# Column strips, split segments and a relaid order in a recurrent-memory attention block with a feed-forward layer

## The chip, the cores and the metric

The kernel runs on one core of a Trainium2 chip. The metric is the device time of one execution in microseconds (us). TensorE (PE; its weight loads are listed as PEld) does the matmuls, VectorE is DVE, ScalarE is ACT, GpSimd is POOL, SyncE (SP) issues transfers. The arrays are in bfloat16, sums in PSUM in float32.

## The reference

`x` has 2048 rows of D = 640. `_A_ref` walks 64 segments of 32 rows. Eight memory rows are put ahead of each segment, attention with 32 heads of 128 runs over these 40 rows, and the first eight rows of its output are the memory of the next segment. So the segments follow one another. `_B_ref` is a feed-forward layer with a squared relu.

```python
for s in range(n_seg):
    h = jnp.concatenate([mem, xs], axis=1)              # 8 + 32 rows
    q, k, v = h Wq, h Wk, h Wv                          # 32 heads of 128
    scores = jnp.einsum('bhqe,bhke->bhqk', q, k) * scale
    scores = jnp.where(mask[None, None], scores, -1000000000.0)
    p = _softmax(scores, axis=-1)
    o = jnp.einsum('bhte,hed->btd', p v, Wo)
    mem = o[:, :M, :].copy()
    outs.append(o[:, M:, :])
...
h = x + _A_ref(_layernorm(x), ...)
h2 = h + _B_ref(_layernorm(h), ...)                     # F = 1728
```

The mask lets the memory rows see all 40 rows, and a segment's row the memory and the rows up to itself.

## The kernel before, in words

There are three phases.

1. Layernorm of all of `x` (L97 to L111): 16 blocks of 128 rows are normalized, transposed on TensorE and written to DRAM as `xnT_dram`. Then the four weight matrices are loaded (L119 to L122), 5 MB each.
2. The recurrence (L140 to L246), a loop over pairs of segments, written as `step`. `hT` holds the transposed rows of a segment, 32 from `xnT_dram` and 8 of memory. For q and k (L154), a block of the weights is the stationary operand (128 x 128) and the 40 columns of `hT` stream through it: 320 weight loads and 320 matmuls of 40 columns. For v (L191), `hT` is stationary (40 columns of the array used) and the weights stream in pieces of 512. Scores are made head by head (L178), scaled and masked on DVE (L180); softmax (L194 to L200) takes the maximum, subtracts, exponentiates on ACT, sums, and multiplies by the reciprocal. The probabilities are transposed (L212), multiplied with v (L220), and Wo is applied with the 40 columns of `oT` stationary (L233). Eight of the result's rows go through `memsb` (L236) and a transpose (L133, L135) into the next segment's `hT`; the others are added to `x` (L240) and written to DRAM as `h1_dram`.
3. The feed-forward layer (L265 to L297): for each block of 128 rows, layernorm, transpose, first product (L281), relu on ACT (L284), square on DVE (L285), second product (L291), bias (L293) and residual (L296).

[...] The framework places the instructions on each engine's queue and adds the semaphores.

Of the kernel before, what the change touches and what calls it, by code (L numbers as in the profile page):

```python
# [16 lines left out]
def kernel(  # L17
# [16 lines left out]
    nc = tc.nc  # L34
# [4 lines left out]
    L = SEG + M  # L39
    NSEG = S // SEG  # L40
    DC = D // 128
    F = B_w1.shape[1]
# [6 lines left out]
    GRP = [(0, 12), (12, 12), (24, 8)]  # L49
    HALF = D // 2  # L50
# [9 lines left out]
    h1_dram = dram.tile([S, D], BF16)  # L60
    xnT_dram = dram.tile([128, DC, S + SEG], BF16)
# [4 lines left out]
    mask = const.tile([L, L], F32)  # L66
    nc.gpsimd.memset(mask[:], 0.0)
    nc.gpsimd.affine_select(out=mask[:, 0:SEG], in_=mask[:, 0:SEG], compare_op=ALU.is_ge, fill=-1e9,
                            base=0, pattern=[[-1, SEG]], channel_multiplier=1)
    mask32 = const.tile([L, H, L], F32)  # L70
    for h in range(H):
        nc.gpsimd.tensor_copy(out=mask32[:, h, :], in_=mask[:])

# [3 lines left out]
    def layernorm(pool, src, n, dst, tagp):  # L77
        xf = pool.tile([128, D], F32, tag=tagp + "xf")
        nc.vector.tensor_copy(out=xf[:n], in_=src)  # L79
        FMAX = nc.vector.BN_STATS_FMAX  # L80
        nsub = 1
        while D // nsub > FMAX or D % nsub:
            nsub += 1
        st = pool.tile([128, nsub, nc.vector.BN_STATS_DIM], F32, tag=tagp + "st")
        xr = xf[:n].rearrange("p (s f) -> p s f", s=nsub)
        for s_ in range(nsub):
            nc.vector.bn_stats(out=st[:n, s_, :], in_=xr[:, s_, :])  # L87
        mv = pool.tile([128, nc.vector.BN_AGGR_DIM], F32, tag=tagp + "mv")
        nc.vector.bn_aggr(out=mv[:n], in_=st[:n])
        rstd = pool.tile([128, 1], F32, tag=tagp + "rs")  # L90
        nc.scalar.activation(out=rstd[:n], in_=mv[:n, 1:2], func=ACT.Sqrt, bias=eps_t[:n], scale=1.0)
        nc.vector.reciprocal(out=rstd[:n], in_=rstd[:n])
        nc.vector.tensor_scalar(out=dst, in0=xf[:n], scalar1=mv[:n, 0:1], scalar2=rstd[:n, 0:1],
                                op0=ALU.subtract, op1=ALU.mult)

    with tc.tile_pool(name="p0", bufs=2) as p0:
        zt = p0.tile([128, DC, SEG], BF16, tag="zt")  # L97
        nc.vector.memset(zt[:], 0.0)
        nc.gpsimd.dma_start(out=xnT_dram[:, :, S:S + SEG], in_=zt[:])
        for g in range(S // 128):  # L100
            xt = p0.tile([128, D], BF16, tag="xt")
            (nc.sync if g % 2 == 0 else nc.scalar).dma_start(out=xt[:], in_=x2d[g * 128:(g + 1) * 128, :])
            xn0 = p0.tile([128, D], BF16, tag="xn0")
            layernorm(p0, xt[:], 128, xn0[:], "ln0")
            pt0 = psum_t.tile([128, 1024], BF16, tag="pt")
            ptv0 = pt0[:, 0:DC * 128].rearrange("p (c m) -> p c m", m=128)
            for c in range(DC):
                nc.tensor.transpose(out=ptv0[:, c, :], in_=xn0[:, c * 128:(c + 1) * 128], identity=ident[:])
            xT0 = p0.tile([128, DC, 128], BF16, tag="xT0")
            nc.vector.tensor_copy(out=xT0[:], in_=ptv0)  # L110
            nc.gpsimd.dma_start(out=xnT_dram[:, :, g * 128:(g + 1) * 128], in_=xT0[:])  # L111

    with tc.tile_pool(name="wts", bufs=1) as wts, tc.tile_pool(name="sb", bufs=1) as sb, \
            tc.tile_pool(name="sm", bufs=2) as sm:
# [4 lines left out]
        nc.sync.dma_start(out=wq[:], in_=A_Wq.rearrange("(c p) h e -> p c (h e)", p=128))  # L119
        nc.scalar.dma_start(out=wk[:], in_=A_Wk.rearrange("(c p) h e -> p c (h e)", p=128))  # L120
        nc.gpsimd.dma_start(out=wv[:], in_=A_Wv.rearrange("(c p) h e -> p c (h e)", p=128))
        nc.sync.dma_start(out=wo[:], in_=A_Wo.rearrange("h e d -> e h d"))  # L122

        hT_a = wts.tile([128, DC, L], BF16)
        hT_b = wts.tile([128, DC, L], BF16)
        memsb = wts.tile([L, D], BF16)
        nc.scalar.dma_start(out=memsb[SEG:L, :], in_=A_mem0[0])

        def mem_to_hT(hT):
            pt = psum_t.tile([128, 1024], BF16, tag="pt")  # L130
            ptv = pt[:, 0:DC * M].rearrange("p (c m) -> p c m", m=M)
            for c in range(DC):
                nc.tensor.transpose(out=ptv[:, c, :], in_=memsb[SEG:L, c * 128:(c + 1) * 128],  # L133
                                    identity=ident[SEG:L, SEG:L])
            nc.vector.tensor_copy(out=hT[:, :, SEG:L], in_=ptv)  # L135

        mem_to_hT(hT_a)
        nc.sync.dma_start(out=hT_a[:, :, 0:SEG], in_=xnT_dram[:, :, 0:SEG])

        def step(t0, off, hT, hT_next):  # L140
            nc.gpsimd.dma_start(out=hT_next[:, :, 0:SEG], in_=xnT_dram[:, :, ds(t0 + (off + SEG), SEG)])
            xs = sm.tile([SEG, D], BF16, tag="xs")
            nc.sync.dma_start(out=xs[:], in_=x2d[ds(t0 + off, SEG), :])

            qT = sb.tile([128, H, L], BF16, tag="qT")
            kT = sb.tile([128, H, L], BF16, tag="kT")
            ei = 0
            for (w_sb, dstT) in ((wq, qT), (wk, kT)):
                for (h0, nh) in GRP:
                    ps = psum.tile([128, 512], F32, tag="mm")  # L150
                    for hl in range(nh):
                        h = h0 + hl
                        for c in range(DC):
                            nc.tensor.matmul(ps[:, hl * L:(hl + 1) * L], lhsT=w_sb[:, c, h * E:(h + 1) * E],  # L154
                                             rhs=hT[:, c, :], start=(c == 0), stop=(c == DC - 1))
                    src = ps[:, 0:nh * L].rearrange("p (h l) -> p h l", l=L)
                    if ei % 2 == 0:
                        nc.vector.tensor_copy(out=dstT[:, h0:h0 + nh, :], in_=src)  # L158
                    else:
                        nc.scalar.copy(out=dstT[:, h0:h0 + nh, :], in_=src)  # L160
                    ei += 1
            v_sb = sb.tile([L, HE], BF16, tag="v")

            HC = 16
            HB = 8
            oT = sb.tile([128, H, L], BF16, tag="oT")
            s = sb.tile([L, H, L], F32, tag="s")
            p = sb.tile([L, H, L], BF16, tag="p")
            pT = sb.tile([L, H, L], BF16, tag="pT")
            mx = sm.tile([L, H], F32, tag="mx")  # L170
            sume = sm.tile([L, H], F32, tag="sume")
            rs = sm.tile([L, H], F32, tag="rsum")
            for b in range(H // HB):
                h0 = b * HB
                ps = psum.tile([128, 512], F32, tag="mm")
                for hl in range(HB):
                    h = h0 + hl
                    nc.tensor.matmul(ps[0:L, hl * L:(hl + 1) * L], lhsT=qT[:, h, :], rhs=kT[:, h, :],  # L178
                                     start=True, stop=True)
                nc.vector.scalar_tensor_tensor(out=s[:, h0:h0 + HB, :],  # L180
                                               in0=ps[0:L, 0:HB * L].rearrange("p (h l) -> p h l", l=L),
                                               scalar=scale, in1=mask32[:, h0:h0 + HB, :],
                                               op0=ALU.mult, op1=ALU.add)
            NVG = HE // 512 // (H // HC)
            for ch in range(H // HC):
                hs = slice(ch * HC, (ch + 1) * HC)
                vps = []
                for n in range(ch * NVG, (ch + 1) * NVG):
                    psv = psum.tile([128, 512], F32, tag="mm", name="vps%d" % n)
                    for c in range(DC):  # L190
                        nc.tensor.matmul(psv[0:L, :], lhsT=hT[:, c, :], rhs=wv[:, c, n * 512:(n + 1) * 512],  # L191
                                         start=(c == 0), stop=(c == DC - 1))
                    vps.append((n, psv))
# [8 lines left out]
                for (n, psv) in vps:  # L202
                    if n % 2 == 0:
                        nc.vector.tensor_copy(out=v_sb[:, n * 512:(n + 1) * 512], in_=psv[0:L, :])  # L204
                    else:
                        nc.scalar.copy(out=v_sb[:, n * 512:(n + 1) * 512], in_=psv[0:L, :])  # L206
# [125 lines left out]
```

## Time and profile before

| | before |
|---|---|
| time, median of 4 | 2596.22 us (2595.84 to 2596.57) |
| profiled span | 2594.5 us |
| TensorE busy | 2155.7 us, 83% |
| DVE busy | 1098.5 us, 42% |
| ACT busy | 607.4 us, 23% |
| mean granted TensorE clock | 0.911 of full speed |

A share of busy time is a mean over phases with different limits. In the rows of groups, `x4096` is the count, then come the total busy time in us, the mean of one in ns, and the idle time of the engine just before. A matmul's listed time runs from its start to its result, so neighbours overlap; what one costs in a row of many is the distance between two starts.

### The profile page before, as it was taken

The numbers are of one execution on the slowest core, as the hardware profiler recorded it, in microseconds if no ns is written. First come the engines' busy times: TensorE is split into PE (matmuls) and PEld (weight loads), VectorE is DVE, ScalarE is ACT, GpSimd is POOL, SyncE is SP. The second block draws the span as 40 slices with busy tenths as digits, with TensorE's granted clock in tenths as the row PEclk, the third lists the DMA queues.
The fourth block names the chain that finished last, engine by engine and source line by source line (L and its number), as shares of the span: only waits on it lengthen the run. The fifth ranks groups of instructions, "written<-read, shape, count | busy, mean of one in ns | idle before, by whom it ended". The sixth has DMA issues, their size and how long they took to land. (4 is left out here: it accounts for less than half of the span.)

```text
span 2594.5 us, 77532 instructions
## 1 busy us (share of the span) xinstructions
PE 2155.7 (83%) x35333; PEld 1568.4 (60%) x35333; DVE 1098.5 (42%) x2262; ACT 607.4 (23%) x1138; POOL 102.5 (4%) x141
## 2 busy tenths in 40 slices
PE   1388889888888888988888888889888888888688
PEld 1266666666566665666666666666666566665465
DVE  6243344433444334444344443344433444334465
ACT  1121222212222122222122221222212222122354
POOL 3000000000000000000000000000000000000011
PEclk9998899888898989989888998899988889989899
DMA  5600000000000000000000000000000000000210
GB/s 178 231 5 6 6 4 5 6 6 6 5 6 6 5 6 6 3 6 6 6 6 5 6 5 6 6 4 5 6 6 6 6 5 6 5 6 13 83 35 29
DMA packets 25770, 49.07 MB, mean 19 GB/s; under 512 B 4984, under 2 KB 21056, under 8 KB 23536
## 3 DMA queue, kind: packets, MB, share of 16 engines
q1 hardware_dynamic: 17984, 24.55, 3.1%
q0 software_dynamic: 3888, 10.70, 1.6%
q10 hardware_dynamic: 3584, 8.78, 0.9%
q8 instruction: 302, 4.95, 0.8%
q14 instruction: 12, 0.10, 0.0%
HBM read 36.10 MB, written 7.91 MB: 17 GB/s over the span
## 5 line engine op out<-in xcount | busy, mean ns | idle before, releaser
L233 PE MATMUL pso<-wo,oT 128*40 128x320 bf16 x4096 | 648.9, 326 | 0.0
L233 PEld LDWEIGHTS <-oT 128*40 128x40 bf16 x4096 | 439.7, 109 | 190.6
L154 PEld LDWEIGHTS <-wq 128*128 128x128 bf16 x10240 | 300.4, 102 | 178.8 <-issue 178.1
L236 DVE CAST memsb<-pso 8x320 bf16<-8x320 f32 x128 | 56.6, 478 | 604.2 <-PE pso L233 604.2
L154 PE MATMUL ps<-hT_a,wq 128*128 128x40 bf16 x5120 | 166.0, 196 | 165.0 <-PEq L244 149.4
L191 PE MATMUL vps<-wv,hT_a 128*40 128x512 bf16 x1280 | 281.4, 379 | 0.0
L191 PE MATMUL vps<-wv,hT_b 128*40 128x512 bf16 x1280 | 281.4, 379 | 0.0
L154 PEld LDWEIGHTS <-wk 128*128 128x128 bf16 x10240 | 264.6, 96 | 0.1
L158 DVE CAST qT<-ps 128x480 bf16<-128x480 f32 (+1 forms) x128 | 73.5, 575 | 395.5 <-PE ps L154 395.5
L206 ACT CAST v_sb<-vps 40x512 bf16<-40x512 f32 x256 | 147.0, 574 | 289.3 <-PE vps L191 289.3
L191 PEld LDWEIGHTS <-hT_b 128*40 128x40 bf16 x1280 | 125.4, 100 | 141.0
L191 PEld LDWEIGHTS <-hT_a 128*40 128x40 bf16 x1280 | 125.4, 100 | 141.0
L160 ACT CAST qT<-ps 128x480 bf16<-128x480 f32 x64 | 35.7, 558 | 656.6 <-PE ps L154 656.6
L204 DVE CAST v_sb<-vps 40x512 bf16<-40x512 f32 x256 | 168.9, 660 | 0.0
L160 ACT ACT_TABLE_LOAD x32 | 41.1, 1283 | 454.1 <-PEq L244 446.8
L154 PE MATMUL ps<-hT_b,wq 128*128 128x40 bf16 x5120 | 137.4, 181 | 11.7 <-DVE hT_b L135 11.7
L154 PE MATMUL ps<-hT_b,wk 128*128 128x40 bf16 x5120 | 135.4, 180 | 0.0
L154 PE MATMUL ps<-hT_a,wk 128*128 128x40 bf16 x5120 | 134.6, 180 | 0.0
L180 DVE SCALAR_TENSOR_TENSOR s<-ps,mask 40x320 f32<-40x320 f32 x256 | 107.3, 475 | 44.7 <-PE ps L178 44.7
L160 ACT CAST kT<-ps 128x480 bf16<-128x480 f32 (+1 forms) x128 | 62.9, 492 | 254.0 <-PE ps L154 254.0
L226 DVE CAST oT<-ps 128x320 bf16<-128x320 f32 x128 | 63.0, 492 | 138.1 <-PE ps L220 138.1
L212 PE MATMUL pt<-ident,p 40*40 40x40 bf16 x2048 | 83.5, 178 | 43.0 <-DVE p L200 43.0
(64 smaller groups left out, 1804.4 us busy)
## 6 DMA issues: line engine op xcount, KB each, us to landing
wq<-in_A_Wq_dram SPq DMA_DIRECT2D x1, 5120.0 KB, 37.6
wk<-in_A_Wk_dram ACTq DMA_DIRECT2D x1, 5120.0 KB, 38.9
wo<-in_A_Wo_dram SPq DMA_DIRECT2D x1, 5120.0 KB, 55.7
wv<-in_A_Wv_dram POOLq DMA_DIRECT2D x1, 5120.0 KB, 40.5
xnT_dram<-xT POOLq DMA_DIRECT2D x16, 160.0 KB, 2.7
xs<-in_A_x_dram SPq DMA_DIRECT2D x64, 40.0 KB, 1.7
h_dram<-h SPq DMA_DIRECT2D x64, 40.0 KB, 1.9
ht<-h_dram SPq DMA_DIRECT2D x16, 160.0 KB, 2.4
```

The lines of the kernel that those rows point to most:

```text
L154: nc.tensor.matmul(ps[:, hl * L:(hl + 1) * L], lhsT=w_sb[:, c, h * E:(h + 1) * E], rhs=hT[:, c, :], start=(c == 0), stop=(c == DC - 1))
L158: nc.vector.tensor_copy(out=dstT[:, h0:h0 + nh, :], in_=src)
L160: nc.scalar.copy(out=dstT[:, h0:h0 + nh, :], in_=src)
L180: nc.vector.scalar_tensor_tensor(out=s[:, h0:h0 + HB, :], in0=ps[0:L, 0:HB * L].rearrange("p (h l) -> p h l", l=L), scalar=scale, in1=mask ...
L191: nc.tensor.matmul(psv[0:L, :], lhsT=hT[:, c, :], rhs=wv[:, c, n * 512:(n + 1) * 512], start=(c == 0), stop=(c == DC - 1))
L204: nc.vector.tensor_copy(out=v_sb[:, n * 512:(n + 1) * 512], in_=psv[0:L, :])
L206: nc.scalar.copy(out=v_sb[:, n * 512:(n + 1) * 512], in_=psv[0:L, :])
L212: nc.tensor.transpose(out=pt2[0:L, hl * L:(hl + 1) * L], in_=p[:, h, :], identity=ident[0:L, 0:L])
L226: nc.vector.tensor_copy(out=oT[:, h0:h0 + HB, :], in_=src)
L233: nc.tensor.matmul(pso[hf][0:L, 0:HALF], lhsT=oT[:, h, :], rhs=wo[:, h, hf * HALF:(hf + 1) * HALF], start=(h == 0), stop=(h == H - 1))
L236: nc.vector.tensor_copy(out=memsb[SEG:L, hf * HALF:(hf + 1) * HALF], in_=pso[hf][SEG:L, 0:HALF])
```

## The change

The change rewrites the recurrence around a narrower stationary operand. It is meant to put four 32-row products into the array side by side and to fill the waits of the recurrence with work that doesn't depend on the memory.

- *Strips.* Heads fall into four groups of eight (G = 4, EG = 1024 columns). The 32 stationary columns of a segment's rows are loaded into four column strips of the array; strip g streams the weights of its own head group and writes PSUM partitions 32g to 32g+31. This holds for q, k and v alike (L185).
- *Split segments.* The 32 stationary rows are the 8 memory rows and the first 24 of a segment (HD = 24). The last eight rows (TL = 8) never feed a later segment's memory other than as keys and values, and their q, k and v don't depend on the memory. The last eight rows of four segments make one 32-row tail pass per block of 128 rows, done one block ahead.
- *Transposes.* q and k are transposed by `turn` (L198), four 128-column transposes at a time.
- *Scores* (L288 to L298): the masks are brought into PSUM by products with the identity, then 64 products of 40 and of 16 columns add the scores. Exp has no subtraction of the maximum. The sums over keys come from a product with a block matrix of ones (L304, L305); the reciprocal is Exp of minus Ln, on ACT.
- *p times v* (L322, L326): 64 products with 32 rows each, in four row groups and four PSUM banks.
- *Wo* for memory and first rows (L338): 16 sets of four strips with 320 columns. This product goes over the even heads alone, and strip g streams the 320 columns of its pair g//2, of which the first 160 are copied out; the odd heads' share of the sum is not formed. As many columns are streamed as 32 heads of 160 would need. Tail rows have all heads (L205).
- *Order.* TensorE's order is as written in the source; `run_fill` takes pieces of the list `fill` (tail passes, their transposes, the tail's Wo, the next block's layernorm transposes) at four places of a step. All 64 steps are written out, without a loop. Layernorm of a block comes just ahead of its use, and its root is Exp of -0.5 times Ln, so that one function table serves all.
- *DRAM.* Attention outputs go to `o_main` and `o_tail`; the feed-forward phase reads them back with `x`, in tiles of 512 rows, w1 stationary and 512 columns streaming.

```diff
-            for (w_sb, dstT) in ((wq, qT), (wk, kT)):
-                for (h0, nh) in GRP:
-                    for hl in range(nh):
-                        for c in range(DC):
-                            nc.tensor.matmul(ps[:, hl * L:(hl + 1) * L], lhsT=w_sb[:, c, h * E:(h + 1) * E],
-                                             rhs=hT[:, c, :], start=(c == 0), stop=(c == DC - 1))
+        def pass_units(w, lhs, n, ps, c0=0, c1=DC):
+            for c in range(c0, c1):
+                for g in range(G):
+                    nc.tensor.matmul(ps[32 * g:32 * g + 32, :], lhsT=lhs(c),
+                                     rhs=w[:, c, g * EG + n * 512:g * EG + (n + 1) * 512],
+                                     start=(c == 0), stop=(c == DC - 1))
...
+        def main_step(b, sp):
+            nc.gpsimd.tensor_copy(out=qT[:, :, :, 0:TL], in_=tl["q"][:, :, :, sp * TL:(sp + 1) * TL])
+            half(wq, lhs, 0, qr, "act")
+            half(wq, lhs, 1, qr, "dve")
+            half(wk, lhs, 0, kr, "act")
+            turn(qr, 0, qT[:, 0:4, :, TL:NQ], "dve")
+            half(wk, lhs, 1, kr, "dve")
+            turn(qr, 1, qT[:, 4:8, :, TL:NQ], "act")
+            half(wv, lhs, 0, vr, "act")
+            turn(kr, 0, kT[:, 0:4], "dve")
+            turn(kr, 1, kT[:, 4:8], "act")
+            half(wv, lhs, 1, vr, "dve")
...
+            p = s1.tile([128, PM + PT], BF16, tag="p")
+            nc.scalar.activation(out=p[:], in_=ps[:, 0:PM + PT], func=ACT.Exp, scale=scale)
+            run_fill(3)
...
+            nc.scalar.activation(out=lz[:], in_=pz[:, 0:PM], func=ACT.Ln)
+            nc.scalar.activation(out=rz[:], in_=lz[:], func=ACT.Exp, scale=-1.0)
+            nc.vector.tensor_tensor(out=pn[:, 0:PM], in0=p[:, 0:PM], in1=rz[:], op=ALU.mult)
...
+            run_fill(5)
...
+            run_fill(3)
+            pw = psum.tile([128, 512], F32, tag="mm", name="pw")
+            for h in range(0, H, 2):
+                for g in range(G):
+                    nc.tensor.matmul(pw[32 * g:32 * g + 32, 0:2 * DG], lhsT=oT[:, h, TL:NQ],
+                                     rhs=wo[:, h, (g // 2) * 2 * DG:(g // 2 + 1) * 2 * DG],
+                                     start=(h == 0), stop=(h == H - 2))
+            o = s3.tile([128, DG], BF16, tag="o", name="o")
+            nc.vector.tensor_copy(out=o[:], in_=pw[:, 0:DG])
+            nc.sync.dma_start(out=o_main[b * 4 + sp], in_=o[:])
+            run_fill(2)
+            if sp < 3:
+                mem_to_hT(o, hT4, sp + 1)
...
-        with tc.For_i(0, S, 2 * SEG) as t0:
-            step(t0, 0, hT_a, hT_b)
-            step(t0, SEG, hT_b, hT_a)
+        for b in range(NB):
+            for sp in range(4):
+                main_step(b, sp)
```

## The prediction

> **What bounds the kernel now.** I read the page first (busy shares, the tenths, the costliest groups), then the stretches of one step, then the order of time at its seams.
>
> ```profile
> span 2594.5 us, 77532 instructions
> ...
> PE 2155.7 (83%) x35333; PEld 1568.4 (60%) x35333; DVE 1098.5 (42%) x2262; ACT 607.4 (23%) x1138; POOL 102.5 (4%) x141
> ...
> PE   1388889888888888988888888889888888888688
> ...
> PEclk9998899888898989989888998899988889989899
> ...
> L233 PE MATMUL pso<-wo,oT 128*40 128x320 bf16 x4096 | 648.9, 326 | 0.0
> ...
> wo<-in_A_Wo_dram SPq DMA_DIRECT2D x1, 5120.0 KB, 55.7
> ```
>
> TensorE is busy 83% of the span and evenly, so the recurrence of 64 segments carries the time, not its ends. The stretches of one step (second segment of a loop body; columns: the stretch, its length, busy time and count on PE, weight loads, DVE, ACT, POOL, then granted clock, DMA share, GB/s):
>
> ```profile
> 999.90:1007.20 7.30, 7.30 (x291) 7.26 (x288) 1.81 (x3) 1.12 (x2) 0.00 (x0) 1.00 0.04 10
> 1007.20:1008.00 0.80, 0.80 (x34) 0.80 (x32) 0.39 (x1) 0.42 (x1) 0.00 (x0) 1.00 0.00 0
> 1008.00:1016.75 8.75, 8.75 (x48) 3.92 (x44) 8.75 (x16) 3.10 (x5) 0.00 (x0) 1.00 0.01 2
> 1016.75:1020.40 3.65, 2.24 (x66) 2.02 (x65) 1.61 (x4) 2.45 (x5) 0.00 (x0) 1.00 0.00 0
> 1020.40:1029.20 8.80, 8.80 (x67) 6.30 (x64) 0.53 (x2) 0.32 (x1) 0.00 (x0) 1.00 0.01 2
> 1029.20:1034.90 5.70, 0.48 (x6) 0.25 (x6) 1.81 (x5) 0.20 (x1) 0.00 (x0) 0.78 0.04 10
> ```
>
> Rows: q and k; scores; v; transposes and p times v; Wo; the seam to the next segment. The loop runs from 104.7 us (first L154 matmul) to about 2392, so 2287 / 64 = 35.7 us a step. Three rates come from it. 160 L154 pairs (weight load and 40-column matmul) take 4.21 us, less 0.18 for the last to finish: 25.3 ns a pair[...], so q and k pay for instructions. 40 V matmuls of 512 columns take 8.75 us: 216 ns each. 64 Wo matmuls of 320 columns take 8.7 us: 135 ns each. In both of these 40 of the array's 128 columns work.
>
> ```profile
> 1003.06 4.21 PE L154 MATMUL ps<-hT_b,wk 128*128 128x40 bf16 x160
> ...
> 1007.20 0.98 PE L178 MATMUL ps<-kT,qT 128*40 128x40 bf16 x32
> ...
> 1029.16 0.89 DVE L236 CAST memsb<-pso 8x320 bf16<-8x320 f32 x2 [8.17 <-PE pso L233]
> 1029.70 0.11 PEld L133 LDWEIGHTS <-memsb 8*128 8x128 bf16 x2 [0.77 <-DVE memsb L236]
> ```
>
> The last L154 matmul starts at 1003.06 + 4.21 - 0.18 = 1007.09, the first L178 at 1007.20: 0.11 instead of 0.025 us, so a change of array shape costs about 0.08 us. DVE to PE takes 0.06 us (1029.16 + 0.48 to 1029.70); a matmul's result reaches ACT or DVE about 0.2 us after the next matmul could start.
>
> ```profile
> 1053.50:1056.90 3.40, 1.92 (x50) 1.55 (x49) 1.87 (x4) 2.29 (x4) 0.85 (x1) 0.91 0.08 12
> 1056.90:1063.70 6.80, 6.79 (x42) 4.29 (x42) 0.49 (x1) 0.42 (x1) 0.00 (x0) 0.54 0.00 0
> ```
>
> After 3.4 us of small matmuls with gaps the clock is halved for 6.8 us.
>
> [...]
>
> **The change part by part.** *Start.* The separate layernorm pass (45 us ahead of the weight loads) goes. Four weight matrices land in about 56 us now; three need 42. From 2 us on that is 44, then the last tail pass (10 sets, 2.2 us): the first step starts at 47 instead of 104.7.
>
> *A step on TensorE.* If four strips run at once, a set of four 512-column matmuls costs 0.216 us, since its eight instructions need only 4 x 25.3 = 101 ns. Per step:
> - 6 half passes of 5 sets: 30 x 0.216 = 6.47, in place of 7.30 + 8.75.
> - 16 transposes of 128 columns at 0.06 (70 L281 matmuls of that width take 4.19): 0.96.
> - Mask and column-sum products, 896 columns: 0.37.
> - 64 score and 64 p-times-v matmuls of 40 or 16 columns, bound by instructions: 128 x 25.3 ns = 3.24.
> - Wo, 16 sets of 320 columns: 16 x 0.135 = 2.16, in place of 8.80.
> - Filler: tail passes, 30 sets in 4 steps, 1.62; tail Wo, 32 sets of 160 columns at 0.101 in 4 steps, 0.81; transposes, 0.3.
> - Memory transposes, 0.1; about 15 shape changes at 0.08, 1.2.
>
> Sum 17.2 us. DVE and ACT beside it: three 512-element evictions at 0.67 and five at 0.58, four 320-element ones at 0.49 and 0.43, exp, Ln and Exp at 0.43 to 0.55: 6 to 7 us each, no bound.
>
> *Waits that the filler leaves.* From scores to p times v: 0.2 + exp 0.55 + sums 0.3 + 0.2 + Ln 0.43 + Exp 0.43 + two multiplies. The multiplies (320 and 128 elements, 16-bit) are not in the trace of before; at the float32 rate of 809 ns for 640 they cost about 0.75,[...] and I take 0.6. That is 2.7 us, against 8 filler units of 1.7 to 2.4: about 0.6 is left. Behind this wait stand, on PE's queue in written order, p times v and all that follows[...]. In two of four steps a filler eviction (0.67) stands behind the multiplies on DVE and frees a PSUM buffer that p times v needs: 0.3 on average. Evictions of p times v (0.2 + 0.49) hide behind up to three units: 0.1. Wo to the next step: 0.2 + copy of 160 elements 0.33 + 0.06, transposes 0.15, 0.2 + copy 0.16 + 0.06: 1.2. Sum 2.2, so 19.4 us. Hidden: the two POOL copies of 256 elements a step and layernorm of the next block, behind projections and Wo.
>
> *Clock.* The stage from scores to p times v streams about 0.75 us in each 1.62 of small matmuls[...]. A halved 6.8 us made Wo take 11.60 instead of 8.87, +2.7. Bounds per step are 0 and 2.7; I take 0.8, as if three steps in ten paid it. Step: 20.2; 64 x 20.2 = 1293.
>
> *Loop removed, DRAM relays.* Straight code ends the 4.6 us stall at each loop end (part of 35.7 already) and the 1.28 us table load there. Writing o to DRAM delays nobody until the end: no step reads it back.
>
> *Feed-forward.* From the loop's end to its first matmul took 24 us (2392 to 2416.3); w1 and w2 again come first. Now four blocks are normalized before the first matmul, three more at about 4 us, less what the missing cast saves: 33. Then 4 tiles of 70 x 0.216 + 112 x 0.135 = 30.2 plus 2 of handover, 129, in place of 178. ACT queues 12 transfers a block ahead of its evictions, at 0.33 us each, which PE's 30 us hide. Total 162.
>
> Sum: 47 + 1293 + 162 = 1502; forecast 1500.
>
> **The rivals.** *Strips run one after another.* Then a step has 120 x 0.216 = 25.9, filler 6.5, Wo 64 x 0.135 = 8.6, tail Wo 2.2, and the other 8.3 us: 51.5; 64 x 51.5 + 209 = 3505, slower. For it: no strip appears in this trace. Against: the weight loads of before overlap running matmuls completely. *Two at a time*: 43.2 / 2 + 8.3 = 29.9 a step, 2120. *The clock stays halved*: some 12 us of streaming (projections, filler, Wo, transposes) take twice as long, 31.4 a step, 2220[...]. *The chain through ACT and DVE is longer than summed*, from engines' own order of filler evictions: +3 us a step, 23.2, 1690. *No clock loss and full hiding*: 18.5 a step, 1390.
>
> **How the numbers follow.** Main case 0.58; longer chain 0.15; no clock loss 0.14; two at a time or clock halved 0.07; one after another 0.06. Faster is all but the last: 0.93; within 0.2% 0.01. The range runs from the no-loss case, 1390, to the longer chain, 1700, and leaves out the three far ones.
>
> **What would show it.** Right: sets of four L185 matmuls starting within a few ns, then 0.216 us apart; steps of 20 us; DVE and ACT under 45%; a clock of 0.9 to 0.95; first step near 47. Wrong: L185 matmuls 0.216 us apart singly (3505), steps of 23 us with PE waiting for rz, pn or pw (longer chain), or a feed-forward part far from 162.

## The result, and the profile after

The changed kernel takes 1366.4 us (median of 8, 1360.9 to 1371.6) where the kernel before takes 2596.5 (median of 12): a ratio of 0.5265, interval 0.5256 to 0.5273. The forecast was 1500 with a range from 1390 to 1700. The direction and the main mechanism, four strips at a time, held. The size was off: 134 us less than forecast, below the range.

The page of the changed kernel, the lines that answer to those of before:

```profile
span 1366.5 us, 57311 instructions
...
PE 1162.4 (85%) x26680; PEld 627.6 (46%) x26680; DVE 454.8 (33%) x1075; ACT 436.9 (32%) x873; POOL 84.3 (6%) x172
...
PE   0179898999899999998999899999999997459998
...
PEclk9999999999999999999999999999999998769999
...
PE 78%; DMA 9%; DVE 7%; ACT 3%; issue 3%; ACTq 0%; SPq 0%
```

TensorE still carries the time, now at 85% of half the span. Three things differ from before. The first slice and a half hold next to no TensorE work, and there is a trough where the recurrence ends and the feed-forward part begins. The clock row, which fell to 8 all along before, stays at 9 until that trough.

The stretches of one step of the changed kernel (columns as before: stretch, length, busy time and count on PE, weight loads, DVE, ACT, POOL, granted clock, DMA share, GB/s):

```profile
441.76:449.91 8.15, 8.15 (x136) 3.74 (x137) 2.79 (x6) 3.38 (x7) 0.00 (x0) 1.00 0.03 7
449.91:450.70 0.79, 0.79 (x71) 0.60 (x68) 0.67 (x1) 0.00 (x0) 0.00 (x0) 1.00 0.00 0
450.70:453.49 2.79, 2.38 (x55) 0.90 (x45) 1.01 (x4) 1.45 (x3) 0.40 (x1) 1.00 0.02 6
453.49:454.16 0.67, 0.67 (x65) 0.62 (x66) 0.08 (x1) 0.00 (x0) 0.00 (x0) 1.00 0.00 0
454.16:454.92 0.76, 0.61 (x17) 0.12 (x10) 0.55 (x2) 0.53 (x2) 0.00 (x0) 1.00 0.00 0
454.92:457.11 2.19, 2.19 (x64) 1.61 (x64) 0.34 (x1) 0.71 (x2) 0.40 (x1) 1.00 0.03 7
457.11:458.32 1.21, 0.47 (x13) 0.20 (x5) 0.52 (x2) 0.00 (x0) 0.00 (x0) 1.00 0.00 0
```

The rows are: q, k and v with their transposes; masks and scores; softmax with eight filler units; p times v; two filler units while its result is copied; Wo; the seam. Together 16.56 us, against 35.7 before. q, k and v fell from 16.05 to 8.15 us, Wo from 8.80 to 2.19 and the seam from 5.70 to 1.21; what lies between, 4.45 before, takes 5.01 with filler in it. No run takes the shorter seam or the split of the segments by itself. Of the four steps of a block, three take 16.6 us and the first, which has the tail's Wo as filler, 18.4. The clock is 1.00 in every row.

TensorE's order of time in the projections and in the two stages of small products now reads as follows (start, duration, engine, line, operands, count; in brackets the idle time before and what ended it):

```profile
441.76 2.34 PE L185 MATMUL ps<-wq,hT 128*32 128x512 bf16 x40 [0.40 <-DVE hT L264]
443.93 1.25 PE L185 MATMUL ps<-wk,hT 128*32 128x512 bf16 x20
...
450.21 0.38 PE L294 MATMUL pss<-qT,kT 128*32 128x40 bf16 x32
450.43 0.44 PE L298 MATMUL pss<-qT,kTt 128*32 128x16 bf16 x32
...
453.49 0.20 PE L322 MATMUL po<-pn,vr 32*128 32x40 bf16 x4 [0.39 <-DVE pn L313]
453.62 0.19 PE L326 MATMUL po<-pn,vt 32*128 32x16 bf16 x4
453.64 0.20 PE L322 MATMUL po<-pn,vr 32*128 32x40 bf16 x4
453.67 0.19 PE L326 MATMUL po<-pn,vt 32*128 32x16 bf16 x4
453.70 0.20 PE L322 MATMUL po<-pn,vr 32*128 32x40 bf16 x4
```

The 40 products of q, ten sets of four strips, begin at 441.76 and those of k at 443.93: 0.217 us a set. L294 begins at 450.21 and L298 at 450.43: 32 small products in 0.22 us. In p times v, after its first group of four (one for each row group), a group begins every 25 to 39 ns. The forecast had 25.3 ns for each single product.

The gain comes from the steps: 35.7 less 17.2 us, 64 times. Against the forecast, time was lost at both ends. The first step ends at 96.96 us (its memory copy, L264), where 67.2 was forecast, and the feed-forward part takes 187.6 us, where 162 was.

### The profile page after: what moved, and what is told of

Its sections match the earlier page's. It is cut to its first block, busy times and chain, and to the rows that moved or that the text cites. A ratio compares the mean times of both kernels' runs of the same rounds, so it can differ in the third digit from the quotient of the medians.

```text
span 1366.5 us, 57311 instructions
## 1 busy us (share of the span) xinstructions
PE 1162.4 (85%) x26680; PEld 627.6 (46%) x26680; DVE 454.8 (33%) x1075; ACT 436.9 (32%) x873; POOL 84.3 (6%) x172
## 4 chain that ended last, share of the span: by engine, by line
PE 78%; DMA 9%; DVE 7%; ACT 3%; issue 3%; ACTq 0%; SPq 0%
PE ps L185 37%; PE pw L338 10%; PE pt L198 7%; PE psf L433 5%; PE psy L446 5%; DMA xt<-in_A_x_dram 3%; PE ps L205 3%; PE po L322 2%; PE po L326 2%; PE pss L294 1%; DVE oT L180 1%; PE pss L298 1%; DVE o L342 1%; DMA wq<-in_A_Wq_dram 1%; DMA wk<-in_A_Wk_dram 1%
## 5 line engine op out<-in xcount | busy, mean ns | idle before, releaser
L185 PEld LDWEIGHTS <-hT 128*32 128x32 bf16 x7680 | 182.5, 97 | 207.3 <-DVE hT L264 31.4
L180 DVE CAST row<-ps 128x512 bf16<-128x512 f32 x160 | 110.6, 691 | 231.0 <-PE ps L185 231.0
L178 ACT CAST row<-ps 128x512 bf16<-128x512 f32 x160 | 94.0, 588 | 291.2 <-PE ps L185 291.2
L185 PE MATMUL ps<-wq,hT 128*32 128x512 bf16 x2560 | 153.2, 386 | 25.9 <-DVE hT L264 25.9
L338 PE MATMUL pw<-wo,oT 128*32 128x320 bf16 x4096 | 163.0, 313 | 12.4 <-DVE oT L180 6.8
L185 PE MATMUL ps<-wv,hT 128*32 128x512 bf16 x2560 | 161.7, 381 | 0.0
L185 PE MATMUL ps<-wk,hT 128*32 128x512 bf16 x2560 | 161.0, 380 | 0.0
L338 PEld LDWEIGHTS <-oT 128*32 128x32 bf16 x4096 | 108.4, 100 | 67.9 <-DVE oT L180 31.8
L198 PE MATMUL pt<-ident,row 128*128 128x128 bf16 x1280 | 111.0, 221 | 15.2 <-DVE row L180 14.9
L198 PEld LDWEIGHTS <-row 128*128 128x128 bf16 x1280 | 72.4, 98 | 98.9 <-issue 80.7
L322 PE MATMUL po<-pn,vr 32*128 32x40 bf16 x2048 | 46.4, 180 | 22.5 <-DVE pn L313 19.1
L322 PEld LDWEIGHTS <-vr 32*128 32x128 bf16 x2048 | 39.7, 91 | 46.3 <-issue 31.2
L185 PEld LDWEIGHTS <-hTt 128*32 128x32 bf16 x1920 | 42.9, 97 | 38.3 <-issue 12.3
```

The costliest lines, as they stand in the source:

```text
L178: nc.scalar.copy(out=out_, in_=in_)
L180: nc.vector.tensor_copy(out=out_, in_=in_)
L185: nc.tensor.matmul(ps[32 * g:32 * g + 32, :], lhsT=lhs(c), rhs=w[:, c, g * EG + n * 512:g * EG + (n + 1) * 512], start=(c == 0), stop=(c = ...
L198: nc.tensor.transpose(out=pt[:, k * 128:(k + 1) * 128], in_=row[:, i * 128:(i + 1) * 128], identity=ident[:])
L322: nc.tensor.matmul(po[g][:, i * NQ:(i + 1) * NQ], lhsT=vr[r, i * E:(i + 1) * E], rhs=pn[r, i * NQ:(i + 1) * NQ], start=True, stop=False, s ...
L338: nc.tensor.matmul(pw[32 * g:32 * g + 32, 0:2 * DG], lhsT=oT[:, h, TL:NQ], rhs=wo[:, h, (g // 2) * 2 * DG:(g // 2 + 1) * 2 * DG], start=(h ...
```

## The experiments

Each changes one thing in the changed kernel (1366.4 us), unless said otherwise. Ratios are to the kernel before in the same runs. The theory after the first reading of the trace: products in different strips or row groups overlap, small ones too (32 of L294 in 0.22 us), so the 25.3 ns floor is one of a place in the array and not of the instruction queue. The rival: something else made the step short, and strips are worth less than they seem.

**e1: small products strip by strip.** All eight heads of one strip, then those of the next, for scores and for p times v.

```diff
-            for i in range(HG):
-                for g in range(G):
+            for g in range(G):
+                for i in range(HG):
...
```

> The 128 small matmuls of a step (scores, p times v) in the order group by group, so that neighbours share a strip. If the 25.3 ns of before is the distance of neighbours in one part of the array, and neighbours in different strips start every 3 to 9 ns, they take 128 x 25.3 ns = 3.24 us instead of about 1.16: +2.1 us a step, 64 times +133: about 1500 us, what the prediction priced. If they are fast for another reason (narrower weight loads, say), order does not matter: 1366.

Measured: 1427.3 us, ratio 0.5499 (0.5485 to 0.5513). Three of the four steps of a block are 1.0 to 1.3 us longer and the first 0.4: on average 0.95, about half of the priced 2.1. The stretches of scores (both kinds) and of p times v in e1, in the same columns as above:

```profile
466.56:467.60 1.04, 1.04 (x69) 1.04 (x71) 0.52 (x1) 0.00 (x0) 0.00 (x0) 1.00 0.00 0
470.31:471.86 1.55, 1.54 (x64) 1.50 (x64) 0.79 (x3) 0.43 (x1) 0.00 (x0) 1.00 0.00 0
```

They took 0.49 and 0.67 us. Inside one strip the starts of e1 are 25 ns apart (25, 26, 25, 25, 25). Near each border two products begin in each 25 ns, one from either strip. So the 25 ns belong to a place in the array, as the theory said. The rest of the price is missing because TensorE took products of the next strip before those of the current one were through. Experiments e6 and e11 follow that.

**e6: five products of a strip in a row, in the projections.** The main passes of q, k and v run strip by strip; the filler's units keep four strips side by side.

```diff
-            for c in range(c0, c1):
-                for g in range(G):
+            for g in range(G):
+                for c in range(c0, c1):
```

> In the projections of a step all five products of one strip come before those of the next strip (strip outer, row block inner); instructions, data and results are the same, and the filler's units keep four strips side by side. If a strip is gained only where neighbours in the queue use different strips, 30 sets a step cost 4 x 0.216 instead of 0.216, +19.4 us a step, 2610 us; where at each of three borders of a half pass the last product of one strip runs beside the first of the next, 3 x 6 x 0.216 = 3.9 less, 2360. If the order doesn't matter (strips queue independently), 1366.

Measured: 1541.8 us, ratio 0.5939 (0.5927 to 0.5951). None of the three numbers. A step is 2.74 us longer, and the starts of one half pass of 20 products show why (ns from the first):

```
0  226 232  442 459 465  658 675 690 696  874 890 906 924  1106 1122 1140  1338 1355  1571
```

One product begins in the first slot of 216 ns, two in the second, three, four, four, three, two, one: eight slots instead of five. Each strip starts one slot after the one before it and then runs beside it. So here TensorE did not work down its queue product by product: a product of another strip went ahead of those that waited for their own. Three slots more in each of a step's four unbroken runs of products are 4 x 3 x 0.216 = 2.6 us.

**e11: ten in a row, for q alone.** Is there a limit to how far ahead it takes them?

```diff
-            half(wq, lhs, 0, qr, "act")
-            half(wq, lhs, 1, qr, "dve")
+            for g in range(G):
+                for n in range(2):
+                    for c in range(DC):
+                        nc.tensor.matmul(pq[n][32 * g:32 * g + 32, :], lhsT=lhs(c), ...
```

> Both half passes of q are made strip by strip: ten products of strip 0, ten of strip 1 and so on, the same work otherwise. In e6, with five in a row, strip s+1 began with the second product of strip s, so a pass of 5 slots took 8. If TensorE takes up to three waiting products of a strip and only then those of the next strip (look-ahead of a fixed depth), strip s+1 begins with the seventh product of strip s, the ten slots become 28, and a step is 18 x 0.216 = 3.9 us longer: 1616 us. If each strip begins one slot after the one before it however long the rows are (no limit on what waits), 13 slots: 1366 + 64 x 3 x 0.216 = 1407, or the changed kernel's order for the half passes of k and v hides it: 1366. If strips never overlap in such an order, 40 slots: 1781.

Measured: 1623.7 us (1621.9 to 1625.5), ratio 0.6257 (0.6245 to 0.6268), next to the 1616 of the fixed look-ahead. Starts of the first eight: 0, 227, 443, 659, 874, 1090, 1306, 1312 ns. In all these runs two such products of one strip lie about 216 ns apart, not 6, so the eighth start is strip 1's first, beside strip 0's seventh, with three of strip 0 still waiting. Where q's last strip ends, the order of time names both lines (L280 is q, L185 is k, which is later in the program):

```profile
613.10 5.62 PE L280 MATMUL pq<-wq,hT 128*32 128x512 bf16 x37 [0.31 <-DVE hT L264]
618.35 0.40 PE L185 MATMUL ps<-wk,hT 128*32 128x512 bf16 x3
618.56 0.38 PE L280 MATMUL pq<-wq,hT 128*32 128x512 bf16 x1
618.58 0.39 PE L185 MATMUL ps<-wk,hT 128*32 128x512 bf16 x3
618.77 0.38 PE L280 MATMUL pq<-wq,hT 128*32 128x512 bf16 x1
```

Three products of k begin ahead of each of q's last three. The 40 products of q need 28 slots instead of 10, from their order alone. That the projections are short because strips run at the same time is thereby shown: the order of one of the three alone costs 257 us.

**e2: Wo over all heads, in 32 sets of 160 columns.** It brings back the odd heads' share of the sum. The forecast had priced a set of four with 160 columns at 4 x 25.3 = 101 ns.

```diff
-            for h in range(0, H, 2):
-                for g in range(G):
-                    nc.tensor.matmul(pw[32 * g:32 * g + 32, 0:2 * DG], lhsT=oT[:, h, TL:NQ],
...
+            wo_units(lambda h: oT[:, h, TL:NQ], pw, 0, H)
```

> Wo of the memory and first rows over all 32 heads, each strip with its own 160 columns: 32 sets of four instead of 16, the same columns, and the sum of the reference is formed. If only columns and the strip distance count, [...]the time stays: 1366 within 0.4%. If eight instructions cost 0.101 us as predicted, the product takes 3.2 instead of 2.2 us: +1.07 a step, 1435.

Measured: 1405.4 us, ratio 0.5416 (0.5405 to 0.5427): between the two. The sets are 0.07 us apart, half of the 0.136 us of a set with 320 columns, as the strip theory has it, yet the time is 39 us longer. The group's row on e2's page:

```profile
L205 PE MATMUL pw<-wo,oT 128*32 128x160 bf16 x8192 | 171.9, 241 | 35.9 <-issue 26.9
```

and one such product in the order of time:

```profile
464.84 2.04 PE L205 MATMUL pw<-wo,oT 128*32 128x160 bf16 x106
467.35 0.59 PE L205 MATMUL pw<-wo,oT 128*32 128x160 bf16 x22 [0.46 <-issue]
```

"issue" is time in which the engine waits for nothing that the profile names. Counted over the Wo, tail Wo and p-times-v runs of the recurrence, neighbours that start more than 0.33 us apart occur 52 times in e2 (49.3 us together) and 22 times in the changed kernel (20.7 us); the idle time of these groups put down to issue is 37.7 and 15.7 us. In the changed kernel every one of these gaps stands at the same place of a count of TensorE's instructions by 256. The pages list a DMA queue q8 of the kind "instruction"; its row on the page of the changed kernel and then on that of e2:

```profile
q8 instruction: 208, 3.41, 1.0%
q8 instruction: 240, 3.93, 1.1%
```

These are packets of 16 KB. The 53 360 products and weight loads of the changed kernel make 256 to a packet, and the 8192 that e2 has more make its 32 more packets. In the dense runs of the changed kernel, where the 128 pairs of such a block are used up in 1.7 to 3.4 us, the next block is mostly late: it starts 0.46 to 2.06 us after the last instruction (a few blocks that were used up as fast show no gap). And each of these late blocks begins 1.20 to 1.55 us after a packet of that queue has landed. So, by these figures, TensorE waits there for its instructions.

The gaps account for 29 of e2's 39 us; the other 10 are not assigned. All 22 gaps of the changed kernel lie in the first steps of blocks, where the tail's Wo is the filler: 1.3 us of the 1.8 by which such a step is longer than the others.

**e9: the whole sum with as few instructions as the changed kernel.** Strips 0 and 2 take the even heads, 1 and 3 the odd ones, 320 columns each; the memory transpose adds the two partial sums through a selector with two ones, and for the other rows POOL adds them in the feed-forward part.

```diff
-                    nc.tensor.matmul(pw[32 * g:32 * g + 32, 0:2 * DG], lhsT=oT[:, h, TL:NQ],
-                                     rhs=wo[:, h, (g // 2) * 2 * DG:(g // 2 + 1) * 2 * DG],
+                    nc.tensor.matmul(pw[32 * g:32 * g + 32, 0:2 * DG], lhsT=oT[:, 2 * hp + g % 2, TL:NQ],
+                                     rhs=wo[:, 2 * hp + g % 2, (g // 2) * 2 * DG:(g // 2 + 1) * 2 * DG],
```

> The whole sum over 32 heads with as many TensorE instructions as the changed kernel: strips 0 and 2 take even heads, strips 1 and 3 odd heads, 320 columns each, and the two partial sums are added by the memory transpose (a selector with two ones) and, for the rows, by a POOL addition in the feed-forward phase. If e2's 39 us come from TensorE waiting for its next block of 256 instructions, they are absent here: 64 x (0.16 for copying 320 instead of 160 columns + 0.03) = 12 and 2 in the feed-forward part, about 1380 us, with idle time of the L338 products put down to issue as low as in the changed kernel. If a full sum costs more for another reason (other data, waits for oT), the time is 1400 or more.

Measured: 1378.8 us, ratio 0.5316 (0.5307 to 0.5326), near the 1380 expected if e2's loss is a wait for instructions. The group's idle time in e9, as its groups by line give it:

```profile
L346 PE MATMUL pw<-wo,oT 128*32 128x320 bf16 x4096 | 158.9, 307 | 13.6 <-DVE oT L184 7.6 <-issue 3.9
```

Issue falls from 26.9 to 3.9 us; the changed kernel has 3.5. The same sum costs 27 us less when it is cut into half as many instructions. With every head in the sum the kernel takes 0.53 of the time of before, so the gain doesn't hang on the heads that the changed kernel leaves out.

**e3: all filler after Wo.** Nothing covers the waits any more.

```diff
-            run_fill(3)
             pz = ...
-            run_fill(5)
...
-            run_fill(2)
+            run_fill(13)
```

> All 13 filler units of a step at its end, none at the waits of softmax and evictions. If the filler hides these waits, about 2.2 us more of them show in a step (0.75 for exp, 1.5 for Ln, Exp and multiplies, 0.7 for evictions, less 0.7 that show already), and the clock may fall as in the kernel before, up to 1.3 more: 1505 to 1590 us. If the waits are hidden otherwise: 1366.

Measured: 1549.5 us, ratio 0.5970 (0.5958 to 0.5982). Softmax with p times v, and then Wo, in e3:

```profile
609.13:613.23 4.10, 1.27 (x89) 0.99 (x79) 1.04 (x5) 1.98 (x5) 0.40 (x1) 1.00 0.00 0
613.23:616.57 3.34, 3.34 (x65) 1.97 (x65) 0.34 (x1) 0.23 (x1) 0.40 (x1) 0.67 0.02 5
```

Two costs show. From scores to Wo TensorE is busy 1.27 of 4.10 us. In the changed kernel this stretch takes 4.22 us (450.70 to 454.92) with the filler in it, so about 2 us of filler no longer lie inside a wait. And Wo, after such a stretch, runs at a clock of 0.67 and takes 3.34 us instead of 2.19. So the filler also pays through the clock: the mean clock of e3 is 0.908, that of the changed kernel 0.971, with the same work in another order.

**e4: DVE and ACT in written order too.** In the changed kernel only TensorE's order is written; the layernorm of the next block is placed on DVE by the framework. DVE at the end of a block's first step, changed kernel:

```profile
711.48 0.33 DVE L342 CAST o<-pw 128x160 bf16<-128x160 f32 x1 [1.06 <-PE pw L338]
712.64 0.49 DVE L109 BATCH_NORM_STATS2 st<-xt 128x6 f32<-128x320 bf16 x1 [0.83 <-DMA xt<-in_A_x_dram]
713.05 0.18 DVE L264 CAST hT<-pm 128x40 bf16<-128x40 f32 x1
```

L109 waits for a block of x, and the memory copy L264, for which all of TensorE waits, stands behind it.

```diff
-            tc.manual_schedule(engines={mybir.EngineType.PE}):
+            tc.manual_schedule(engines={mybir.EngineType.PE, mybir.EngineType.DVE, mybir.EngineType.Activation}):
```

> DVE and ACT also in the order of the source, so that layernorm statistics that wait for a transfer no longer stand ahead of an eviction or of the copy of the memory. If that is what makes the first step of a block 18.5 us instead of 16.6, it falls to about 17.3, and some 8 us go from the start: 1366 - 18 - 8 = 1340. If the first step is longer through TensorE's own work (32 sets of the tail's Wo): 1366.

Measured: 1348.4 us, ratio 0.5194 (0.5186 to 0.5203). That is between the two expected times, nearer to 1340. The first steps of the blocks (without the first and the last block) fall from 18.36 to 17.73 us, and the first memory copy after a step moves from 96.96 to 90.29; in the changed kernel, in e4 and in e5 it is:

```profile
96.96 0.20 DVE L264 CAST hT<-pm 128x40 bf16<-128x40 f32 x1 [0.42 <-PE pm L262]
90.29 0.20 DVE L264 CAST hT<-pm 128x40 bf16<-128x40 f32 x1 [0.42 <-PE pm L262]
78.26 0.20 DVE L266 CAST hT<-pm 128x40 bf16<-128x40 f32 x1 [0.45 <-PE pm L264]
```

**e5: no layernorm behind the weights.** On top of e4, three x blocks go ahead of the weights, later ones are loaded one block earlier, and the weights are issued from SP and POOL instead of SP and ACT.

```diff
+        load_x(1)
+        load_x(2)
...
-                (nc.sync if c % 2 else nc.scalar).dma_start(out=w[:, c, :], ...
+                (nc.sync if c % 2 else nc.gpsimd).dma_start(out=w[:, c, :], ...
```

> The written queue order of e4 is kept (1348 us); three x blocks are loaded ahead of the weights, the weights are issued from SP and POOL so that ACT's queue holds none of them, and later x blocks are loaded one block earlier. If the late start comes from ACT and DVE standing behind transfers, only the weights' own arrival is left: 20.9 MB at the 310 GB/s of the changed kernel's first slices are 68 us, so the second copy of memory columns moves from 90.3 to about 72 us, and the time is 1330. The sp0 steps, whose layernorm waits for x, lose up to 0.8 us each in 15 blocks, another 0 to 10. If the start is bound by the transfers alone, nothing moves: 1348.

Measured: 1342.3 us (1337.1 to 1345.5), ratio 0.5175 (0.5166 to 0.5183): 6 us below e4, not 18. The copy after the first step comes at 78.3 instead of 90.3, where 72 was expected, since in this order wv's last part lands later:

```profile
58.26 1.05 PE L187 MATMUL ps<-wv,hTt 128*32 128x512 bf16 x8 [1.81 <-DMA wv<-in_A_Wv_dram]
```

In the changed kernel a landing of wv ends ACT's idle time at 50.11 us (shown below). So the start is bound by both: the order on the queues gave 19 us of it between the changed kernel and e5, and the weights' arrival holds what is left. In the profiled run, the fastest of its four, the last step still comes 11 us earlier than in e4; why the median keeps 6 of them stays open.

**e7: w1 and w2 a step earlier.** They go into the buffers of wq and wk during the last step.

```diff
+            if b == NB - 1 and sp == 3:
+                nc.sync.dma_start(out=w1, in_=B_w1.rearrange("(c p) f -> p c f", p=128))
+                nc.gpsimd.dma_start(out=w2[:, 0:FFULL, :], ...
```

> The changed kernel, but w1 and w2 go into the buffers of wq and wk as soon as the last step has used these, issued from SP and POOL, so that they stand ahead of no load of the feed-forward phase. If the phase's 35.6 us before its first product are lengthened by x loads standing behind w2 (9 us until the first x block could be added), 10 to 15 us go: 1353 us. If the chain of four layernorm blocks alone sets them, nothing moves: 1366.

Measured: 1357.0 us, ratio 0.5222 (0.5212 to 0.5233). The first product of the feed-forward part comes 22.4 us after the recurrence instead of 35.6. Of these 13 us, 9 stay: the last block's steps take 4 us longer, at a lower granted clock (0.77 against 0.91 from 1122 to 1141 us, before the weights are issued), which isn't explained.

**e10: e4, e5, e7 and the whole sum of e9 together.**

> The whole sum over 32 heads of e9 (1378.8) with the written order of e4 (-18), the transfers of e5 (-6) and the early w1 and w2 of e7 (-9); the normalized block has one buffer instead of two. If the four act in different stretches of the time they add: 1346 us. If e4 and e5 shift work onto the stretch that e7 shortens, or the wider copy of o stands behind other work in the written order of DVE, 1355 to 1365.

Measured: 1348.0 us (1347.2 to 1350.7), ratio 0.5195 (0.5188 to 0.5202). The gains add nearly in full: 31 us less than e9, where the single runs give 33. So they lie, for the most part, in different stretches. This version forms the sum over all 32 heads and still takes 1.3% less time than the changed kernel and 48% less than the kernel before.

## Why the prediction was right or wrong

Right: the loop of 64 steps carries the time; four strips of 512 columns, whose running at once was an assumption that no run of before shows, last as long as one product (sets of L185 216 ns apart, single starts in a set 3 or 4 ns); Wo's 16 sets take 2.19 us (2.16); DVE and ACT stay at 33% and 32%; ACT loads one function table in the whole span (1.28 us), 34 before. The waits were forecast at 2.2 us and are, in the step shown, 0.21 and 0.57 around softmax, 0.31 before Wo and 1.1 at the seam: 2.2. A change of shape costs 0.09 us (0.08); the two 16-bit multiplies 0.32 and 0.22 us, 0.54 together (0.6, the author's estimate). Strips one after another and two at a time are refuted by the set distances, and e6 and e11 show what such orders would cost.

The step that failed is *a step on TensorE*, in its terms "128 x 25.3 ns = 3.24" and "32 sets of 160 columns at 0.101". The 25.3 ns had been read off 160 pairs that all used the whole array, and I took them for the cost of an instruction. In strips and row groups four go in that time.

| per step, us | forecast | measured |
|---|---|---|
| 128 small products | 3.24 | 0.22 + 0.27 + 0.67 = 1.16 |
| tail Wo, quarter of 32 sets | 0.81 | 32 x 0.069 / 4 = 0.55 |
| clock | 0.8 | 0 in the steps shown |
| mean step | 20.2 | 17.17 |

The three terms make 3.14 us, where the whole is 3.03; the instruction gaps of e2's kind (20.7 us in all, 0.3 a step) go the other way and were not in the forecast. The small products are settled by e1, the sets of 160 columns by e2's own distances.

*Clock* was a guess between 0 and 2.7 us, and came out at the lower end. The rival of a clock that stays halved is out with the 1.00 of the rows above; in the kernel before, too, the stretch at 0.54 (1056.9 to 1063.7 us) was followed by one at 1.00 (1063.7 to 1067.1). A likely reason is that the thin stage is short and well filled: small products that take a third of the time leave the stage from scores to p times v 85% busy (2.38 of 2.79). e3 shows the loss that was feared, where the filler is moved. That a clock loss is absent for this reason and no other was not tested further. In the last block, which has no filler left, the clock does fall (0.50 in its last Wo).

*Start* was 30 us short (67.2 against 96.96 for the first step's end). Some 8 of these are the transfers themselves: 15.7 MB, the size of three matrices, had come in at 51.7 us, at the 308 and 321 GB/s of the page's first two slices, where the forecast had 44 us from the faster rate of before. The larger part is that I didn't ask what stands on the queues that issue them. On ACT in the changed kernel:

```profile
43.05 7.01 ACTq L155 DMA_DIRECT2D wo<-in_A_Wo_dram  x2
50.11 0.29 ACT L113 ACTIVATE lv<-mv,eps_t 128x1 f32<-128x1 f32 x1 [48.09 <-DMA wv<-in_A_Wv_dram]
```

The first layernorm's root waits 48 us behind transfers that ACT issues, the first product comes at 51.1, and the tail passes that should have run while wk and wv landed begin only then. Then DVE waits 16.88 us for the second block of x, which lands behind wo, with an eviction behind that wait:

```profile
69.44 1.28 DVE L109 BATCH_NORM_STATS2 st<-xt 128x6 f32<-128x320 bf16 x3 [16.88 <-DMA xt<-in_A_x_dram]
...
71.10 0.67 DVE L180 CAST row<-ps 128x512 bf16<-128x512 f32 x1
```

e4 and e5 together take 19 of the 30 us away, so that the order on the queues is the cause is shown for that part.

*Feed-forward* was 26 us short. Its preamble took 35.6 (33 forecast). ACT issues x behind w2, whose issue holds its queue for 8.5 us:

```profile
1179.63 8.49 ACTq L389 DMA_DIRECT2D w<-in_B_w_dram  x1
...
1188.16 0.78 ACTq L409 DMA_DIRECT2D xt<-in_A_x_dram  x1
```

e7 takes both this issue and the transfers of w1 and w2 out of the preamble, which is then 13 us shorter; which of the two counts wasn't tested. The four tiles took 152 instead of 129: the trace has 1.6 us a tile of shape changes at the 64-row remainder of F (8 times 0.2), 4.0 us instead of 2 between tiles, and a clock of 0.50 for 3.4 us in the first sets after three of these pauses (from 1252.6, 1290.1 and 1327.7 us). No run separates these.

The sum by these measures: 1502 + 30 - 63 x 3.03 + 26 = 1367. The steps were 191 us too long in the forecast, and both ends 56 too short: that the total is off by no more than 134 is luck. Of the rivals, "no clock loss and full hiding" (1390) was nearest, for half of its reason: the clock loss was absent, the waits were not.

## What to carry to other kernels

The distance between two instructions read off the profile was here the limit of the place that both used (25 ns inside one strip, 32 products in 0.22 us over four); before such a distance is multiplied by a count, ask whether the new work uses the same place, and give strips the price divided by their number as the other bound. When work moves onto straight code with many short products, look for "issue" idle time at equal distances of 256 instructions: fewer, wider products did the same sum in less (e9: 3.9 us of such time, e2: 26.9). And for each engine, list what stands on its queue behind transfers that it issues or waits for: this cost 19 us at the start, and another order took it away.

## What was not expected of the hardware

- TensorE started products out of program order where they lie in different strips (e1, e6, e11): with five of a strip in a row each strip started one slot of 216 ns late, with ten, six slots late, and three waiting products of a strip were passed by.
- Four strips at 512 columns keep 216 ns a set in 30 sets a step, a gain of four over the 216 ns of one such product before.
- Dense short products outran the instruction supply of this straight code: 0.46 to 2.06 us at a block's boundary, 20.7 us in the changed kernel and 49.3 in e2; in the changed kernel each late block begins 1.20 to 1.55 us after a packet of the instruction queue.
